# Sharing out one DMA engine's rows in six stores of an attention backward kernel

## The chip, the cores and the metric

The kernel runs on one core of a Trainium2 chip. The metric is the time of one execution on the device, in microseconds. The core has 16 DMA engines, which all its queues share; they are numbered 0 to 15 here, so "the fifth" is engine 4.

## The reference

For each of 64 heads (batch 2 by 32) there is one query row of 128 numbers and 8192 rows of keys and of values, all in bf16. The outputs are the attention's result and the gradients of query, keys and values:

```python
def _fwd_reference(q, k, v):
    scale = q.shape[-1] ** -0.5
    scores = jnp.einsum("bhqd,bhkd->bhqk", q, k) * scale
    p = _softmax(scores, axis=-1)
    return jnp.einsum("bhqk,bhkd->bhqd", p, v)
...
    _out, _vjp = jax.vjp(_f, q, k, v)
    _grads = _vjp(grad_out)
```

With one query row, a head's gradient of the values is an outer product (weights by the row of grad_out), and that of the keys another (score gradients by the query row). So the kernel reads 2 MB of keys and 2 MB of values for each head and writes two gradients of the same size: 268 MB each way.

## The kernel before

A head's keys, or its values, are one buffer of 128 partitions by 64 rows of 128 numbers, 16 KB in each partition. There are ten such buffers, `ring` (L108). A loop over heads and eight steps `j` writes the order of all work out by hand. In each step TensorE transposes blocks of keys or values (L144), ScalarE or VectorE copies them to bf16 (L151, L149), and TensorE multiplies them with the query and grad_out (L160). Softmax and its gradient follow on small tiles. VectorE then writes the outer products over the loaded rows, in the same buffer (`outer`, L317), and the buffer is stored as the gradient. So a buffer is loaded, read, overwritten, stored, and loaded again.

`load` (L121) issues a load of 2 MB from SyncE's queue SP. `store` (L361) issues a store of 2 MB from ScalarE's queue, at the end from SP. `cleared` (L123) issues the next load into the buffer just stored, which waits for the store's landing. An ordinary load or store gives each of the 16 DMA engines eight partitions' rows.

Six of the 128 stores are done otherwise: those with 2h+w in 10, 30, 50, 70, 90, 110 (`is_rare`, L134). For them `store` calls `store_by_fifteen` (L335), which cuts the store into 21 DMAs from GpSimd's queue (POOL). In these no row goes to engine 4; its eight partitions (16 to 19 and 48 to 51) are given to other engines, two at a time. Such a buffer is loaded again only after ten further stores (`AWAY`), behind a small DMA (`between`, L114).

A DMA of n rows from POOL goes to n engines that follow each other, starting where the one before ended. So the kernel keeps count of this starting point. It moves the point on, where needed, by tiny transfers of n rows into a tile that nobody reads (`turn`, L326). Whole-row transfers (`size=16384`) of four rows go to engines 0 to 3 and leave the point where it is. For each r of 0 to 3, with the entry e of EXTRA, the store by pieces does this:

```python
            rows(20 + r, 3)                    # engines 5, 6, 7
            rows(r, 4, size=16384)             # engines 0 to 3
            rows(96 + r, 8)                    # engines 8 to 15
            rows(32 + r, 4, size=16384)        # engines 0 to 3
            if e:
                turn(e)                        # point from 0 to e
            rows(16 + r, 2, step=32)           # engine 4's two rows: to e and e + 1
            for n in (9, 8) if e == 2 else ((3 - e) % 16,):
                turn(n)                        # point back to 5
```

The comments are added here. `rows(52, 44, 1)` ahead of the loop gives four rows each to engines 5 to 15, and `turn(5)` brings the point past 0 to 4.

Of the kernel before, what the change touches and what calls it, by code (L numbers as in the profile page):

```python
# [18 lines left out]
RARE = 20  # L19

EXTRA = (
    (0, 5, 8, 10), (2, 7, 11, 13), (0, 6, 9, 14), (2, 5, 9, 12), (0, 7, 11, 13), (2, 5, 8, 14),
)
RING = 10
AWAY = 10
# [504 lines left out]
```

## Time and profile before

| | |
|---|---|
| Median of 3 runs | 1275.2 us (1275.2 to 1276.61) |
| The profiled execution, its own time | 1275.3 us |
| Its span, first to last instruction | 1273.5 us |
| Mean granted TensorE clock | 0.94 |
| Busy: PE, ACT, DVE, POOL | 85%, 76%, 70%, 8% |
| Bytes moved | 539.01 MB, mean 423 GB/s |
| Issue to landing, median: load, store from ACT | 38.8 (keys) and 38.6 (values), 19.3 us |
| Issue to landing, median: the two-row piece of POOL | 22.8 us |

The profile shows one execution. Its span is 1.8 us shorter than the execution's time; that part lies around the instructions. The line of tenths for DMA is the busy share of all 16 engines together. The share of a queue is the time that its packets took, as a share of 16 engines over the span. "Issue to landing" ends when the last of the engines that have a part in the DMA is done with it.

### The profile page before, as it was taken

Reading aid. Unit: us, or ns where it says so; the run is one execution under the profiler, and the core shown is the slowest. Engines: PE = TensorE matmul, PEld = TensorE weight load, DVE = VectorE, ACT = ScalarE, POOL = GpSimd, SP = SyncE. Lnnn points to the kernel's source line nnn. Section 1 sums busy time; section 2 is a strip of 40 time slices with the busy share of each in tenths; the row PEclk is TensorE's granted clock in tenths of the full one; section 3 lists DMA queues with packets and bytes.
Section 4 is the critical chain, followed back from the end, with each engine's and each line's share of the span. In section 5 each row is a group of like instructions: output and inputs, shape, how many; then the busy total and the mean of one; then the engine's idle time right before and its main releaser. Section 6 shows DMA issues by size and latency. Waiting matters only on the chain.

```text
span 1273.5 us, 31594 instructions
## 1 busy us (share of the span) xinstructions
PE 1083.4 (85%) x13444; PEld 721.0 (57%) x13444; DVE 891.6 (70%) x1574; ACT 971.1 (76%) x1134; POOL 106.9 (8%) x194
## 2 busy tenths in 40 slices
PE   5999998769988869888888888888888888898895
PEld 4666665546655546555565555555555555565563
DVE  1888886658766658776667677677676776776685
ACT  5898886758877759777778777777786777787785
POOL 1001110001110000211000121000111000022000
PEclk9999998889998989899889998999898999898997
DMA  9999999999999999999999999999999999999997
GB/s 393 419 428 429 425 427 427 428 430 428 426 426 426 430 429 427 427 427 426 430 429 427 430 426 426 428 429 428 426 424 426 426 428 429 425 414 426 428 415 333
DMA packets 44552, 539.01 MB, mean 423 GB/s; under 512 B 10682, under 2 KB 10682, under 8 KB 10682
## 3 DMA queue, kind: packets, MB, share of 16 engines
q1 hardware_dynamic: 20026, 285.22, 52.7%
q10 hardware_dynamic: 16736, 239.15, 44.2%
q0 software_dynamic: 7648, 12.61, 2.6%
q8 instruction: 105, 1.72, 0.5%
q14 instruction: 37, 0.30, 0.1%
HBM read 268.47 MB, written 268.47 MB: 422 GB/s over the span
## 4 chain that ended last, share of the span: by engine, by line
DMA 75%; PE 16%; ACT 4%; DVE 3%; issue 1%; ACTq 0%; SPq 0%; DVEq 0%
DMA ring<-in_k_dram 51%; DMA ring<-in_v_dram 15%; PE tp L144 9%; DMA out_dram<-ring 7%; ACT ev L151 4%; PE raw L160 2%; PE acc L285 2%; DVE ring L317 2%; PE turned L177 2%; DMA spare<-in_q_dram 1%; DMA nat<-in_grad_out_dram 1%; DVE rawsb L171 1%; DVE ev L149 0%; PE misc L229 0%; ACT E_f L218 0%
## 5 line engine op out<-in xcount | busy, mean ns | idle before, releaser
L151 ACT CAST ev<-tp 128x1024 bf16<-128x1024 f32 x960 | 936.3, 1017 | 288.4 <-PE tp L144 237.8
L144 PE MATMUL tp<-ident_bf,ring 128*128 128x128 bf16 x8192 | 661.0, 226 | 151.0 <-DMA ring<-in_k_dram 67.4
L144 PEld LDWEIGHTS <-ring 128*128 128x128 bf16 x8192 | 516.2, 101 | 370.1 <-issue 239.8
L317 DVE TENSOR_TENSOR ring<-qd,dS 128x2048 bf16<-128x2048 bf16 (+1 forms) x256 | 305.4, 1214 | 0.3 <-PE acc L285 0.3
L317 DVE TENSOR_TENSOR ring<-qd,P 128x2048 bf16<-128x2048 bf16 x255 | 305.3, 1218 | 0.1
L171 DVE COPY rawsb<-raw 128x512 f32<-128x512 f32 x127 | 87.8, 692 | 236.2 <-PE raw L160 235.0
L285 PE MATMUL acc<-ring,wz 128*32 128x512 bf16 x2048 | 211.2, 404 | 1.4 <-DVE wz L232 1.4
L160 PE MATMUL raw<-ev,qz 128*4 128x512 bf16 x2048 | 205.1, 390 | 0.1
L341 POOL DMA_DIRECT2D out_dram<-ring x126 | 70.7, 562 | 959.8 <-DVE ring L317 610.8
L177 PE MATMUL turned<-ident_f,rawsb 128*128 128x128 f32 x512 | 90.7, 305 | 11.6 <-DVE rawsb L171 10.2
L149 DVE CAST ev<-tp 128x1024 bf16<-128x1024 f32 x64 | 78.4, 1225 | 16.3 <-PE tp L144 15.7
L160 PEld LDWEIGHTS <-qz 128*4 128x4 bf16 x2048 | 46.6, 81 | 56.4 <-issue 6.2
L177 PEld LDWEIGHTS turned<-ident_f,rawsb 128*128 128x128 f32 x512 | 60.6, 154 | 26.7 <-DVE rawsb L171 25.3
L285 PEld LDWEIGHTS <-wz 128*32 128x32 bf16 x2048 | 52.7, 93 | 30.6 <-issue 3.0
L229 PEld LDWEIGHTS misc<-ld,ones_f 128*128 128x128 f32 x256 | 38.6, 190 | 15.2 <-DVE ld L256 10.9
L229 PE MATMUL misc<-ld,ones_f 128*128 128x1 f32 x256 | 46.1, 249 | 0.4 <-DVE ld L256 0.4
L209 DVE TENSOR_REDUCE gm<-misc 1x1 f32<-1x128 f32 x64 | 17.8, 279 | 38.5 <-PE misc L207 38.5
L331 POOL DMA_DIRECT2D spare<-in_q_dram x56 | 33.0, 588 | 120.3 <-DMA out_dram<-ring 102.3
L203 DVE TENSOR_REDUCE mp<-turned 128x1 f32<-128x64 f32 x64 | 14.1, 220 | 25.1 <-PE turned L177 23.9
L215 DVE TENSOR_SCALAR negm<-misc 128x1 f32<-128x1 f32 x64 | 9.8, 153 | 24.1 <-PE misc L213 24.1
L213 PE MATMUL misc<-gm,ones_f 1*128 1x1 f32 x128 | 24.2, 256 | 0.0
L213 PEld LDWEIGHTS misc<-gm,ones_f 1*128 1x128 f32 x128 | 18.7, 183 | 6.8 <-issue 0.4
(46 smaller groups left out, 283.1 us busy)
## 6 DMA issues: line engine op xcount, KB each, us to landing
out_dram<-ring ACTq DMA_DIRECT2D x114, 2048.0 KB, 19.3
ring<-in_k_dram SPq DMA_DIRECT2D x64, 2048.0 KB, 38.8
ring<-in_v_dram SPq DMA_DIRECT2D x64, 2048.0 KB, 38.6
out_dram<-ring SPq DMA_DIRECT2D x5, 2048.0 KB, 20.3
out_dram<-ring SPq DMA_DIRECT2D x6, 1024.0 KB, 10.7
out_dram<-ring POOLq DMA_DIRECT2D x6, 704.0 KB, 15.2
out_dram<-ring POOLq DMA_DIRECT2D x48, 64.0 KB, 21.1
out_dram<-ring POOLq DMA_DIRECT2D x24, 128.0 KB, 22.3
```

The source lines that it names most:

```text
L144: nc.tensor.matmul(tp[:, i, :], lhsT=x.kv[w][:, n, :], rhs=ident_bf[:], start=True, stop=True)
L149: nc.vector.tensor_copy(out=ev[:], in_=tp[:])
L151: nc.scalar.copy(out=ev[:], in_=tp[:])
L160: nc.tensor.matmul(raw[32 * k : 32 * k + 4, :], lhsT=qz[w][:, at : at + 4], rhs=evs[k // 2][:, 4 * (k % 2) : 4 * (k % 2) + 4, :].rearrange ...
L171: copy(out=x.raw[:], in_=raw[:])
L177: nc.tensor.transpose(out[:, i], x.raw[:, i * P : (i + 1) * P], ident_f[:])
L213: nc.tensor.matmul(mb, lhsT=ones_f[0:1, :], rhs=x.gm[:], start=True, stop=True)
L229: nc.tensor.matmul(x.lsum, lhsT=ones_f[:], rhs=x.ld[:, w : w + 1], start=True, stop=True)
L285: nc.tensor.matmul(acc[32 * g : 32 * g + 32, :], lhsT=wz[w][:, n // 4, at : at + 32], rhs=rows[:, n : n + 4, :].rearrange("p n d -> p (n d)"),
L317: nc.vector.tensor_tensor(out=x.kv[1 - w][:, n : n + size, :].rearrange("p n (d t) -> p n d t", t=2), in0=row.unsqueeze(1).to_broadcast([P ...
L331: nc.gpsimd.dma_start(out=two(spare[0:n, :])[:, :, i : i + 2], in_=two(q_rows[0:n, :])[:, :, 0:2])
L341: nc.gpsimd.dma_start(out=dst[own], in_=src[own], max_dma_last_dim=size)
```

## The change

Only the table EXTRA changes, the entry e for each of the six stores and each r:

```diff
 EXTRA = (
-    (0, 5, 8, 10), (2, 7, 11, 13), (0, 6, 9, 14), (2, 5, 9, 12), (0, 7, 11, 13), (2, 5, 8, 14),
+    (0, 5, 6, 10), (2, 6, 5, 5), (0, 5, 6, 14), (2, 6, 5, 5), (0, 6, 5, 12), (2, 6, 5, 6),
 )
```

Entries of 0 and 2 stay, so engines 0 to 3 get the same rows of the fifth's as before. Of the other 36 rows, 30 go to engines 5, 6 and 7, none to 8 and 9, and one each to 10 to 15. The `turn` calls around them have other sizes, in the same number.

## The prediction

> **What bounds the kernel now.** I read the page from its slices down, then the waits of the queue that issues the loads, then the trace's single DMA packets.
>
> The page's slices and queues:
>
> ```profile
> DMA  9999999999999999999999999999999999999997
> ...
> q1 hardware_dynamic: 20026, 285.22, 52.7%
> q10 hardware_dynamic: 16736, 239.15, 44.2%
> q0 software_dynamic: 7648, 12.61, 2.6%
> q8 instruction: 105, 1.72, 0.5%
> ```
>
> All slices but the last are at 9: the DMA engines are full from start to end. q1 carries the loads (and the last stores), q10 the stores, q0 the stores by pieces, q8 the fetch of instructions. The chain of waits by engine, and the longest waits of SP's queue, which issues the loads:
>
> ```profile
> DMA 75%; PE 16%; ACT 4%; DVE 3%; issue 1%; ACTq 0%; SPq 0%; DVEq 0%
> ```
>
> ```profile
> SPq L121 <- DMA out_dram<-ring: 563.9, 63, 28.7
> ```
>
> Loads wait for stores to free a buffer, and the chain waits for loads. A DMA has landed only when all 16 engines have done their part, so the question is which engine is last. The mean over 16 engines hides that; the end of the run shows it. The DMA view of the window from 1262 to 1273 us, in 40 slices:
>
> ```profile
> DMA  9989999998899999999854425655533322000000
> GB/s 387 387 357 387 417 477 447 477 477 358 358 447 447 387 417 447 477 387 357 291 216 179 209 121 245 248 246 213 210 157 124 129 123 91 30 30 0 0 0 0
> ```
>
> From slice 20 (1267.5 us) on half the engines are done, the other half work on to 1272 us. Which half: the packet records name queue, start, duration and size, not the engine, but on one engine a packet starts 3 or 4 ns before its predecessor ends, and every engine takes 8 rows and one 4-byte count of each load. So the 44,563 packets can be strung into 16 chains. In each of the 126 DMAs by pieces, a chain shows data where the engine has rows and 4-byte placeholders where it has none; each chain up to the last load fits the pattern that EXTRA and the turns give for one engine number, with no DMA that disagrees (0 and 1, and 2 and 3, are told apart only as pairs). What the chains show:
>
> - All 105 fetches of 16 KB on q8 fall on engines 5, 6, 9, 10, 11, 12, 13 and 14, in this order in turn, 13 each (12 has 14). A fetch takes 0.95 us in the mean, and the three packets after it are 0.41 us longer than usual: 1.36 us, 17.7 us an engine over the run. The other eight have none.
> - These eight are never idle from the first 10 us to 1233 us, the last load's landing; the others are, late in the run.
> - Position at the last load (issued at 1211.0 us), in us ahead of the last engine: 14 0.00, 6 0.65, 9 0.90, 13 1.62, 12 1.87, 5 1.92, 11 2.90, 10 2.96, then 3 8.0, 0 8.7, 4 10.3, 2 11.7, 1 12.7, 15 13.7, 8 13.9, 7 14.8. The landings of the last store have much the same form: eight within 1.95 us (0, 0.55, 0.64, 0.91, 1.59, 1.61, 1.64, 1.95), then a gap to 4.7.
>
> So the end of the run is the sum of the work of the last fetching engine, now 14, with 6 close behind.
>
> **The change part by part.** Issues and turns stay: the same 126 pieces and 56 turns, and a turn of e and its counterpart still move 19 engines in all (3 where e is 0). POOL's issue rows (561 and 578 ns) and their order stay, and so does the count of packets on q0. SP, ACT, PE and DVE have no instruction changed. I cost all this at nothing. What hides small differences on POOL is the time between the last piece's landing and the reload of its buffer: 33.4, 27.8, 30.1, 27.6 and 30.8 us for the first five (213.9 to 247.4 us for the first); the sixth has no reload. A store by pieces that takes 27 us longer would cost from there on, microsecond for microsecond.
>
> What moves is 48 rows. Counted from EXTRA (an entry e gives one row to e and one to e+1), before and after: 0 to 3 three each, both times; 5: 3 to 8; 6: 4 to 15; 7: 3 to 7; 8 and 9: 4 to 0; 10, 11, 12, 13: 3 to 1; 14: 4 to 1; 15: 2 to 1.
>
> One such row is two packets of 8192 bytes at 309 ns (median of 1152): 0.618 us; a placeholder that it replaces took 9 ns, 6 of them its own. By engine:
> - Engine 6: +11 rows = 6.80 us, less 22 x 0.006 = 0.13: +6.67 us. It is a fetching engine without idle time, so nothing hides it but its lead of 0.65 us: +6.0 us past the old end.
> - Engine 5: +5 rows = +3.0 us, less its lead of 1.92: +1.1, behind engine 6, so nothing by itself.
> - Engine 14: -3 rows = -1.8; 13 and 12: -1.2; 9: -2.4; 10 and 11: -1.2. All are ahead of engine 6 then, and their gain is idle time.
> - Engine 7: +2.4 us, against a lead of 14.8: nothing. Engines 8 and 15 had leads already: nothing.
>
> Does lateness on one engine reach the end one to one? Upper bound: all 6.7 us, if its lead is used up elsewhere. Lower bound: its lead was 2.7 us three loads earlier (at load 123), before its last fetch at 1215 us; with that, and with nothing made up in the tail, +4.0. I take 6.0, because the eight engines were still close together, and apart from the rest, at the last store. The depth of loads in flight feeds engine 6 always:
>
> ```profile
> ring<-in_k_dram SPq DMA_DIRECT2D x64, 2048.0 KB, 38.8
> ring<-in_v_dram SPq DMA_DIRECT2D x64, 2048.0 KB, 38.6
> ```
>
> 38.8 us from issue to landing is what the slowest engine needs; at 784 us the first engine had its share after 16.5. An engine 6 us later still has tens of us queued, and those ahead only idle more.
>
> Sum: the profiled execution took 1275.3 us (span 1273.5, 1.8 around it); the median of the runs is 1275.2. 1275.2 + 6.0 = 1281.2.
>
> A rule that looks at the same engines: the Trainium skill, DMA: Bandwidth & Descriptors, section Latency and other measured facts, says that engines 7 and 15 are usually the slower ones in traces. By it the sum would be that of the last rival below, 1277.7. Here both are among the three that lead at the last load, so the measurement decides against it for this case.
>
> **The rivals.**
> - *Fetching falls on other engines in the changed program.* The profile has one execution; the set of eight could be given anew with each program. If 5 and 6 fetch nothing, they have about 10 us or more of lead, the rows are free, and the last engine is one of 9 to 14 with 2 to 4 rows less, or 15 with one less: -0.6 to -2.5 us, 1272.7 to 1274.6, likeliest 1274.0. For it: nothing in the code fixes the set. Against it: the set held through 105 fetches in strict turn, and the program's length doesn't change. 0.10 for a result within 0.2%. The faster side needs more: the last engine must be 8 or 9 (four rows, 2.5 us, 1272.7) and other things go well. 0.04.
> - *Lateness is partly made up.* In the tail the chain runs through PE from 1211 to 1251 us; if stores are issued later than engine 6 asks for work, its backlog drains meanwhile: +2 to +4, 1277.2 to 1279.2. Against it: the eight kept their distances to the end. 0.09.
> - *The pieces take longer and hold their buffer past its reload.* The wait would be the reload's on the last piece. Each of POOL's DMAs waits for the eighth before it (latency 21 to 23 us, some 30 DMAs, so four rounds); with 2 or 3 more rows on engine 6, up to 1.9 us a round, 7 us in all against 27.6 of cover. It decides from 27.6 us on; with ten more it would be 1291. 0.01.
> - *Engine 7 is last after all*, by a slower row than 611 ns: four rows, 1275.2 + 2.5 = 1277.7. It would need 14.8 us of lead gone. 0.01.
>
> **How the numbers follow.** Forecast 0.75 (its own range 1279.2 to 1282.5: bounds of 4.0 and 6.7, and some tenths of scatter, as the runs before spread 1.4). With it slower by over 0.2%, 2.6 us, about what a measurement of this kernel can tell from no change: most of the partly-made-up case and the last two, together 0.85. Same 0.11: new fetch set and a small rest. Faster 0.04. The range 1276.5 to 1283.5 leaves out the new fetch set (0.14) and the reload case.
>
> **What would show it.** In the trace after: 105 fetches on the same eight engines; from the second half on, each load's last landing alone, some 4 to 6 us after the second last (0.6 to 2.7 before); engine 6 the last chain, with 30 half rows of the fifth's rather than 8; the last stores 5 to 7 us later, the DMA slices at the end thinning to one engine in 16 rather than eight; loads' landing time about as before. Wrong it would be if another engine were last, if engine 6 fetched nothing, or if engine 6 were last by 6 us and the end still where it was.

## The result, and the profile after

The changed kernel takes 1280.68 us (median of 6 runs, 1280.18 to 1281.33), against 1275.32 us for the kernel before, measured alongside (6 runs, 1275.17 to 1276.61). The ratio is 1.0041, with a 95% interval of 1.0028 to 1.0054: slower, by 5.4 us, where the prediction had 6.0. The profiled execution took 1280.18 us, the least of the six; its span is 1278.4 us (4.9 more than before), and its mean granted clock is 0.944, as before.

The page's slices and queues, in the same places as before (queue: packets, MB, share of 16 engines):

```profile
DMA  9999999999999999999999999999999999999997
...
q1 hardware_dynamic: 20026, 285.22, 52.5%
q10 hardware_dynamic: 16736, 239.15, 44.1%
q0 software_dynamic: 7648, 12.61, 2.6%
q8 instruction: 105, 1.72, 0.5%
```

Packets and bytes of every queue are the same to the last one; only the shares of the longer span have gone down. Nothing in these lines says where 4.9 us went, which is why the prediction went below them. The chain of waits by engine, and the longest wait of SP's queue (total, times, longest):

```profile
DMA 77%; PE 15%; ACT 4%; DVE 3%; issue 1%; ACTq 0%; SPq 0%; DVEq 0%
```

```profile
SPq L121 <- DMA out_dram<-ring: 531.7, 63, 28.6
```

The chain has gone from 75% to 77% of DMA. The loads' time to landing, which the prediction said would stay, did:

```profile
ring<-in_k_dram SPq DMA_DIRECT2D x64, 2048.0 KB, 38.6
ring<-in_v_dram SPq DMA_DIRECT2D x64, 2048.0 KB, 38.8
```

What answers to the window that showed half the engines at work until the end is the DMA view of the window from 1267 to 1278 us, again in 40 slices of 0.275 us:

```profile
DMA  9999999698999994411111110111000000000000
GB/s 417 387 477 477 477 447 387 268 447 357 477 477 477 447 417 164 105 42 62 60 61 61 61 61 0 60 61 62 33 30 30 30 0 30 30 30 0 0 0 0
```

Fourteen engines are done with the bulk of their work by slice 17 (1271.7 us). Then the rate is 60 GB/s, and from slice 28 on 30 GB/s: two engines, then one. Before, eight engines ran out together. Strung into chains as in the prediction, the packets say which they are. In us ahead of the last, at the last load: engine 6 0, engine 5 2.1, then six between 6.0 and 7.5 (10 to 13, one of the pair 8 and 9, one of the pair 14 and 15), then nothing up to 11.9. (The two of such a pair can't be told apart in this run, as their rows are the same; the one counted here carries 13 fetches, the other none.) The 16 landings of the last store say the same: 0, 2.16, 5.51 and closely on. It landed at 1277.37 us, before at 1272.50: +4.87, which is the whole difference of the spans.

### The profile page after: what moved, and what is told of

It reads as the page before. It is cut to its first block, busy times and chain, and to the rows that moved or that the text cites. A ratio compares the mean times of both kernels' runs of the same rounds, so it can differ in the third digit from the quotient of the medians.

```text
span 1278.4 us, 31594 instructions
## 1 busy us (share of the span) xinstructions
PE 1077.5 (84%) x13444; PEld 715.3 (56%) x13444; DVE 891.0 (70%) x1574; ACT 971.6 (76%) x1134; POOL 107.1 (8%) x194
## 4 chain that ended last, share of the span: by engine, by line
DMA 77%; PE 15%; ACT 4%; DVE 3%; issue 1%; ACTq 0%; SPq 0%; DVEq 0%
DMA ring<-in_v_dram 40%; DMA ring<-in_k_dram 30%; PE tp L144 8%; DMA out_dram<-ring 5%; ACT ev L151 4%; PE acc L285 2%; PE raw L160 2%; DVE ring L317 2%; PE turned L177 2%; DMA spare<-in_q_dram 1%; DMA nat<-in_grad_out_dram 1%; DVE rawsb L171 1%; PE misc L229 0%; ACT E_f L218 0%; PE misc L303 0%
## 5 line engine op out<-in xcount | busy, mean ns | idle before, releaser
L317 DVE TENSOR_TENSOR ring<-qd,dS 128x2048 bf16<-128x2048 bf16 (+1 forms) x256 | 305.4, 1215 | 0.3 <-PE acc L285 0.3
## 6 DMA issues: line engine op xcount, KB each, us to landing
ring<-in_k_dram SPq DMA_DIRECT2D x64, 2048.0 KB, 38.6
ring<-in_v_dram SPq DMA_DIRECT2D x64, 2048.0 KB, 38.8
```

What stands on the lines that cost most here:

```text
L317: nc.vector.tensor_tensor(out=x.kv[1 - w][:, n : n + size, :].rearrange("p n (d t) -> p n d t", t=2), in0=row.unsqueeze(1).to_broadcast([P ...
```

## The experiments

One theory stood against several rivals. **Theory:** the end is set by the engine with the most work, and the eight that carry instruction fetches have no spare time. A row of the fifth's costs 0.612 us there: two half rows, each starting 306 ns after the one before. **Rivals:** what counts is how many rows are piled on few engines, or on engines 5 to 7, or the lateness is partly made up, or the pieces hold their buffers longer, or the fetches have nothing to do with it.

### The same rows on two engines without fetches: e1_seven_eight

```diff
-    (0, 5, 8, 10), (2, 7, 11, 13), (0, 6, 9, 14), (2, 5, 9, 12), (0, 7, 11, 13), (2, 5, 8, 14),
+    (0, 7, 7, 7), (2, 7, 7, 7), (0, 7, 7, 7), (2, 7, 7, 7), (0, 7, 7, 7), (2, 7, 7, 7),
```

> The entries of EXTRA other than 0 and 2 are all 7: the 36 rows go to engines 7 and 8, 18 each (before 3 and 4); none to 5, 6 and 9 to 15. More on one engine than the change put on engine 6 (15). My theory (an engine that fetches instructions is last and never idle, one that fetches none has lead to spare): 7 and 8 have 14.8 and 13.9 us of lead at the last load and get 15 and 14 rows more, at 0.612 us 9.2 and 8.6 us, which they take from their lead. The fetching engines lose 3 or 4 rows each; the last, 14, loses 4: 2.4 us faster, 1272.9 us where the kernel before takes 1275.3. Rival (whichever engine gets the pile is last, or rows on 5 to 7 cost time as such): 3 rows more in the pile than in the change, 5.4 + 1.8 us slower, 1282.5; by the count of rows on 5 to 7 alone (8 more, against 20 more and 5.4 us in the change) 2.2 slower, 1277.5.

Measured: 1272.84 us, ratio 0.998 (0.9972 to 0.9989). Engines 7 and 8 have 18 rows each, more than engine 6 in the changed kernel, and the kernel is faster than before. Engine 14 is last again at the last load and has lost its 4 rows, 4 x 0.612 = 2.45 us. The median is 2.45 us below that of before (1275.29), the last load landed 2.8 us earlier and the last store 2.5. So it isn't the crowding of rows on few engines that costs, but which engines they are.

### More rows on engine 6: e2_six_seven

```diff
+    (6, 6, 6, 6), (6, 6, 6, 6), (6, 6, 6, 6), (6, 6, 6, 6), (6, 6, 6, 6), (6, 6, 6, 6),
```

> All 24 entries of EXTRA are 6: engines 6 and 7 get all 48 rows of the fifth's, 24 each (before 4 and 3, in the changed kernel 15 and 7). My theory: engine 6 has 9 rows more than in the changed kernel, 9 x 0.612 = 5.5 us: 1280.7 + 5.5 = 1286.2 us; engine 7 stays ahead with as many rows. The last two landings of each late load are 10 us or more apart. Rival (lateness of one engine is partly made up, the more the later it is): less than half of that, 1281.5 to 1283.5.

Measured: 1287.58 us, ratio 1.01 (1.0086 to 1.0114), 12.3 us more than before for 20 rows more on engine 6. That is 1.4 more than expected, from only four runs that spread from 1286.87 to 1291.05. The DMA view of the window from 1273 to 1284 us:

```profile
DMA  9999969999989799999935000000000000000000
GB/s 477 447 417 387 387 268 477 477 477 477 447 328 387 328 447 447 477 477 447 417 128 126 35 32 30 0 31 31 31 31 30 31 0 31 31 31 30 30 0 0
```

From slice 22 on there is one engine, at 30 GB/s, for 4.4 us. Engines 6 and 7 have the same 24 rows here; at the last load one of them is last and the other is 13.35 us ahead of it. The last one carries 13 fetches, the other none. This is the cleanest pair of the study: equal rows, one engine at the end and the other among the leaders.

### A few rows on engine 6, the rest as before: e6_six_ten

```diff
+    (6, 5, 8, 10), (6, 7, 11, 13), (6, 6, 9, 14), (6, 5, 9, 12), (6, 7, 11, 13), (6, 5, 8, 14),
```

> The table of before with its six entries of 0 and 2 changed to 6: engine 6 gets 10 rows (before 4), engine 7 gets 9 (before 3), 0 to 3 get none; 5 and 8 to 15 keep theirs. My theory: 6 rows more on engine 6, 3.7 us, less its lead of 0.65 us: 3.0 us, 1278.3; as the changed kernel fell 0.6 us short of the same sum, 1277.7 is as likely. The rows that 8 to 15 lost in the change play no part, so this lies on one line of 0.612 us a row with the changed kernel. Rival (the change was slower by something else in its table, such as the pairs that share engine 5 and 6, or what 8 to 15 no longer take): no change, 1275.3.

Measured: 1277.48 us, ratio 1.0016 (1.0007 to 1.0025). Engine 6 has 10 rows rather than 4 and is last, 2.4 us behind 9 and 14. No other fetching engine was relieved, so what the change gives those is not part of the price: it is engine 6's rows alone (engine 7 gets six as well, and leads by 14.9 us). The rise is 2.2 us, 0.8 less than the sum's 3.0; the change itself also fell short, by 0.6 (below).

### Fewer fetches: e3_fewer_fetches and e4_fewer_fetches_after

One matmul writes its block into the places of two, so TensorE has 9348 matmuls and as many weight loads to fetch, 18696 instructions rather than 26888:

```diff
-        for i in range(HC):
+        for i in range(0, HC, 2):
...
-                tp[:, i, :], lhsT=x.kv[w][:, n, :], rhs=ident_bf[:], start=True, stop=True
+                tp[:, i : i + 2, :], lhsT=x.kv[w][:, n, :],
+                rhs=ident_bf[:].unsqueeze(1).to_broadcast([P, 2, P]), start=True, stop=True
```

e3_fewer_fetches has this with the table of before, e4_fewer_fetches_after with the changed table.

> The kernel before, with half of the transposes left out: one matmul writes the transpose of one block into the places of two, so half of the scores are those of other rows. TensorE's program has 4096 matmuls and 4096 weight loads less; nothing else is changed, no DMA of the kernel either. My theory (the fetches make the eight engines late): 8192 instructions of 64 bytes are 32 fetches of 16 KB, so some 73 rather than 105, 4 less for each of the eight engines, at 1.36 us: 5.4 us faster, 1269.9. Rival (those eight are late for another reason, or the bound isn't on them): as TensorE isn't the bound, 1275.3, or up to 1.5 us less by a shorter tail.

> The changed kernel with half of the transposes left out, as in fewer_fetches (half of the scores are those of other rows). My theory: engine 6 is last here and has 4 fetches less, 4 x 1.36 = 5.4 us less than the changed kernel's 1280.7: 1275.3, so that the change costs the same 5.4 us over fewer_fetches (1269.7) as over the kernel before. Rival (fetches of the other seven engines matter for the changed kernel too, or PE's shorter program hides the rows): below 1273.

Measured: e3 1269.71 us, ratio 0.9954 (0.9942 to 0.9967), and e4 1275.34 us, ratio to before 1.0001 (0.9992 to 1.001). The page of e3, engines' work and fetches:

```profile
PE 1074.3 (85%) x9348; PEld 570.6 (45%) x9348; DVE 891.1 (70%) x1574; ACT 970.6 (77%) x1134; POOL 106.9 (8%) x194
...
q8 instruction: 73, 1.20, 0.3%
```

PE is busy 9 us less of 1083, its weight loads (PEld, beside the matmuls) 150 less, DVE and ACT as before. The fetches have gone from 105 to 73, four fewer on an engine: 256 of TensorE's instructions to a fetch in both. Four times 1.36 us is 5.4; the kernel gained 5.6, and its last store landed 5.75 us earlier (1266.75 against 1272.50). The experiment also changes the form of the transposes, so by itself it leaves room for a cause on TensorE. What speaks against that is e4, with the same TensorE instructions. There engine 6 is last again, 3.4 us behind engine 5 at the last load. From 12 us on until then there is no gap over 50 ns between its packets, nor was there in the changed kernel, so a faster TensorE could not have brought its end forward. It has the same rows as there and 9 fetches rather than 13, and the kernel takes 5.3 us less than the changed one. From e3 to e4 the change costs 5.6 us, from before to after 5.4. In e4's window from 1262 to 1273 us the tail of one engine is there again, from slice 21 (1267.8 us) to the end:

```profile
DMA  9999998989999251101100000000000000000000
GB/s 477 477 477 447 417 387 357 417 357 477 477 477 447 78 138 65 61 30 60 38 32 31 30 31 0 31 31 31 30 30 30 30 30 0 30 30 30 0 0 0
```

A rule of the Trainium skill, Runtime: NRT & Kernel Launch, section Instruction fetch mechanics, says that the cost of crossing a 16 KiB boundary in the instructions is mostly hidden. For this kernel it isn't, since the fetch takes the time of a DMA engine that has none to spare (5.6 us for 32 fetches).

### Rows moved away from the fetching engines: e5_away_from_fetch

If the theory holds, the pieces should start where the fetches are not. EXTRA becomes a table of starts, and all of a piece's rows can go elsewhere (`go(place)` issues the turn from the present point, and `spare` is twice as wide):

```diff
-        for r, e in enumerate(EXTRA[(2 * h + w) // RARE]):
+        for r, (a, b, e) in enumerate(EXTRA[(2 * h + w) // RARE]):
+            go(a)
             rows(20 + r, 3)
             rows(r, 4, size=16384)
+            go(b)
             rows(96 + r, 8)
             rows(32 + r, 4, size=16384)
-            if e:
-                turn(e)
+            go(e)
             rows(16 + r, 2, step=32)
```

> A version made after this reading: the stores by pieces give rows away from the eight engines that fetch (5, 6, 9 to 14). Besides the fifth's rows, all to 7, 8, 15 and 0 now, eight of the 24 steps start their rows of 5 to 7 or of 8 to 15 at another engine. Against the kernel before, engine 9 has 12 rows less, 14 has 10, 10 to 13 have 9, 6 has 6, 5 has 5; 0 has 11 more, 1 has 10, 2 and 3 have 6, 4 has 9, 7 and 8 have 12 and 11, 15 has 4. My theory: 14 stays about last and has 10 rows less, 6.1 us: 1269.2; the engines that get rows have 8 to 15 us of lead at the last load and take at most 7.3. Rival (one of those, or the pieces with some more turns, becomes the bound before that): no better than seven_eight, 1272.8 or more.

Measured: 1273.44 us, ratio 0.9981 (0.9972 to 0.999): a gain of 1.8 us, where I expected over 6; the rival came true, one of the receivers became the bound. The theory wasn't at fault, but my use of it was. At the last load engine 1, one of those that received rows, was last, and the next 2.4 us ahead. It had a lead of 8.66 us before (by its fetches on q14 it is the one put down as 0 of the pair 0 and 1 there) and got 10 rows more, 6.1 us. I had counted that as room enough; but by the same sum the last fetching engine had moved forward by 6 us meanwhile, so engine 1's own end, 8.66 - 6.1 = 2.5 us earlier than the old one, had become the kernel's. By that sum the time is 1272.8, and 0.6 us are left without a cause.

### A table worked out by leads: e7_by_work and e8_spare_four

The same program as e5_away_from_fetch, with starts chosen so that each engine's lead before, less its new rows, comes out as equal as could be found.

```diff
-    ((15, 1, 7), (5, 8, 7), (2, 1, 7), (5, 8, 15)),
...
+    ((5, 8, 15), (7, 8, 7), (13, 8, 15), (5, 15, 7)),
...
```

> The program of away_from_fetch with another table, worked out as a sum for each engine: its lead at the last load in the kernel before, less 0.612 us for each row more (0.632 on engine 4). Rows against the kernel before, engines 0 to 15: +12, +6, +5, +5, +8, -6, -7, +12, +10, -7, -9, -9, -9, -7, -8, +4. By that sum engines 1, 2, 3, 6 and 14 are last together, each 4.9 to 5.0 us earlier than engine 14 was: 1275.3 - 4.9 = 1270.4. The same sum gives 1272.8 for away_from_fetch, with engine 1 last (8.66 us of lead, 10 rows more), where 1273.4 was measured and engine 1 was last. Rival (rows by pieces are dearer than 0.612 us, by the turns and the longer stores): no better than 1272.8.

Measured: 1272.73 us, ratio 0.9976 (0.9967 to 0.9985), 2.3 us short of the sum and at the rival's number. Up to the last load the sum was exact: it landed at 1228.5 us, before at 1233.4, that is 4.9 earlier, with eight engines within 1.1 us. But the last store landed only 2.7 earlier. The DMA view from 1260 to 1271 us shows one engine alone from slice 25 on (1266.9 us):

```profile
DMA  9799999978677767755566432000000000000000
GB/s 387 328 417 447 447 447 417 477 328 324 250 298 298 298 275 309 309 226 211 211 276 276 159 153 89 30 30 30 30 30 30 30 30 0 0 0 0 0 0 0
```

It is engine 4, which was 0.3 us ahead at the last load. Its rows take longer than the others', 616 against 607 ns for a load's and 633 against 607 for a store's (medians before, start to start), and the tail has only stores. So e8_spare_four gives engine 4 fewer rows:

```diff
-    ((5, 8, 15), (7, 8, 7), (13, 8, 15), (5, 15, 7)),
...
+    ((5, 2, 7), (7, 8, 7), (7, 10, 2), (15, 8, 7)),
...
```

> The program of e7_by_work with another table of starts. Rows against the kernel before, engines 0 to 15: +12, +6, +5, +5, +5, -6, -7, +11, +9, -6, -8, -8, -8, -7, -8, +5. Engine 4 gets 5 rows more instead of 8, because in e7_by_work its rows, on average 27 ns longer, let it fall back 2.2 us behind the others between the last load and the last store, where it was last alone. Theory (the busiest engine sets the end, each row 0.612 us, and a receiver must have its lead plus what the others gain): the engine that would be last is 9, 0.9 us ahead of the last one before and 6 rows less, together 4.6 us: 1275.3 - 4.6 = 1270.7 us. Rival (something other than engine 4's slower rows holds the tail): no better than e7_by_work, 1272.7 us.

Measured: 1271.52 us, ratio 0.9969 (0.9958 to 0.998), the best table here, some 4 us faster than before and 9.2 than the changed kernel. It lies between theory and rival: 0.8 us above the one, 1.2 below the other, and its interval overlaps that of e7_by_work. The traces tell more than the times. In the window from 1259 to 1270 us the tail is gone:

```profile
DMA  9999989899998887557868755653222110000000
GB/s 477 447 447 417 447 357 417 357 447 477 447 447 329 326 336 298 238 242 308 339 248 334 301 222 214 251 215 149 119 119 89 60 60 0 0 0 0 0 0 0
```

The last two engines end 0.11 us apart (4 and one of the pair 2 and 3), the next 0.58 ahead. So the traces bear out that engine 4's slower rows made e7's tail; the times alone don't show it, as their intervals overlap, and other engines' rows changed too. But at the last load one of 2 and 3 was last, not 9 as in the sum; 9 was 0.5 us ahead of it, 4.4 earlier than the old end where the sum had 4.6. The one of 2 and 3 carries fourteen smaller fetches of another queue (q14, 4.3 us in all), and the one with as many had a lead of 8.0 us before; less 5 rows, 3.1 us, it should have ended 5.0 us earlier than the old end, and it ended 3.9 earlier. That 1.1 us, like the 0.6 of engine 1 in e5_away_from_fetch, stays open: engines that receive rows end somewhat later than their lead less the rows.

## Why the prediction was right, and where not

- **The set of fetching engines stayed.** 105 fetches again, on 5, 6, 9 to 14, for all that the chains can tell; the same eight in e8_spare_four, where no fetching engine has the same rows as one without fetches. The rival that another set would be given has nothing for it in any of these runs.
- **Engine 6 last.** Right: last at every load from the 95th on, with 30 half rows of the fifth's. The others' gain was idle time, as forecast: the engines with fewer rows, 14 among them, are 6.0 us and more ahead, and the end didn't follow them.
- **The size.** Measured +5.4 by the medians and +4.9 in the profiled executions, against 6.0. The step that was off is engine 6's +6.67 us. Its chain to the last load is 4.20 us longer than before. In it the 22 half rows are 6.73 us rather than 6.80 (a packet starts 306 ns after the one before; I had taken its duration, which overlaps by 3 or 4 ns), and the placeholders -0.13 as forecast. One fetch of instructions is missing (-1.17: the 13th came at 1249 us instead of 1215, after the last load), and everything else, above all the rows of loads and stores, is 1.23 shorter together. About 0.4 of that goes with the missing fetch, whose three next packets would have been longer. The fetch came back in the tail, with 1.36 us: 5.6 for engine 6 at the end, less its lead of 0.65, is the 4.9 measured. So the row's size, 0.612 for 0.618, is only 0.07 of what was off. The larger part, about 0.8 us, is that engine 6's other rows, some 2,000, took less in sum than before, where the prediction had them unchanged. Why is open: on engine 6 of e6_six_ten they took 0.8 less too, and its time fell short of the sum by as much, while e2_six_seven came out above it (12.3 measured, 20 x 0.612 - 0.65 = 11.6).
- **The distances.** "Some 4 to 6 us after the second last" held for most loads from the 95th to the 123rd (5.6 at load 100, 6.8 at load 121). It did not from the 64th to the 94th, where it was 1.0 to 4.2, nor at the end, where it was 2.1. I had engine 5 at 3.0 - 1.9 = +1.1 and so 4.9 behind engine 6. While loads and stores still alternate on an engine, a lead is seen two to three times as large, I think because a row of a store lies between any two of a load (no run tried that); as the queues ran out, 6.8 became 2.1, and the third engine's 11.7 became 6.0. A distance has to be read at one place of the run to be compared.
- **The last stores "5 to 7 us later".** 4.87: just outside, for the reason given under the size. The slices thinned to two engines and then to one, as forecast.
- **Lateness partly made up.** Refuted: 11 rows cost 5.4, 20 cost 12.3, and loads took 38.6 and 38.8 us to land, as before.
- **Pieces that hold their buffer.** Refuted: between the last piece's landing and the reload lie 33.4, 27.5, 30.8, 27.8 and 33.3 us, before 33.4, 27.8, 30.1, 27.6 and 30.8.
- **Engine 7 last.** Refuted: 14.6 us ahead at the last load in the changed kernel, and with 18 rows in e1_seven_eight still 6.9 (7.2 for engine 8). The rule of the Trainium skill on engines 7 and 15 that the prediction names found no support here: their rows start every 607 ns as those of the others do, engine 4 aside.

## What to carry to other kernels

Where all DMA engines are full, ask which one has the most to do and not how busy they are in the mean: here half a per cent more work on one of sixteen (11 rows, 6.7 us of 1275) cost 5.4 us, with no packet or byte more in all. Rows and fetches of instructions go into one sum, and the end of the run shows in the DMA slices how many engines are last. When work is moved off the busiest, an engine that receives must keep its lead after the others have moved forward too, and the sum must be made for the very end, not for the last load.

## What the runs showed of the hardware

- TensorE's instruction fetches of 16 KB ride on the same 16 DMA engines as the data and fell in turn on the same eight of them in every kernel here whose chains tell, about 13 each: 1.36 us a fetch, 17.7 us an engine. At the last load of the kernel before, every engine without them led by about 8 us or more.
- Engine 4 is slower than the rest with the same rows, by 9 ns on a load's row and 26 on a store's. In the kernel before it had no rows of the six stores by pieces and none of the 16 KB fetches, and its lead over the last engine there was 10.3 us.
